# A new emission order, explicit waits at the port that VectorE and GpSimd share, and a plan that keeps DMA issue and DMA data apart, in a fused local-attention and feed-forward kernel

## The chip, the cores and the metric

The kernel runs on one core of a Trainium2 chip. The metric is the device time of one execution in microseconds (us); lower is better. A core has five engines that run instruction streams of their own: TensorE (PE, matmuls), VectorE (DVE), ScalarE (ACT), GpSimd (POOL) and SyncE (SP). In this kernel SyncE computes nothing: it issues every DMA. Engines wait for each other through semaphores.

## What is computed

```python
B, H, S, D = q.shape
block, window = (32, 16)
...
k_sum = k.reshape(B, H, nb, block, D).max(axis=3)
v_sum = v.reshape(B, H, nb, block, D).mean(axis=3)
scores_l = scale * np.matmul(q, k.transpose(0, 1, 3, 2))
...
mask_l = np.abs(pos[:, None] - pos[None, :]) < window
scores_s = scale * np.einsum('bhsd,bhnd->bhsn', q, k_sum)
scores_s = scores_s + np.log(block)
scores_l_m = np.where(mask_l, scores_l, -1000000000.0)
scores_all = np.concatenate([scores_l_m, scores_s], axis=-1)
...
a = a / (np.sum(a, axis=-1, keepdims=True) + 1e-09)
v_all = np.concatenate([v, v_sum], axis=2)
return np.matmul(a, v_all).astype(np.float32)
...
h = x @ w_in
g = h * (1.0 / (1.0 + np.exp(-h)))
return (g @ w_out).astype(np.float32)
```

There are 4 batches, 8 heads, 768 tokens and 64 elements in a head; `a` is the exponential of the scores less their maximum.

The attention output, laid out as 3072 tokens by 512, is the input x of the feed-forward part (FFN). All data is float32.

## The kernel before

**Work and tiles.** Products are made in float16: each float32 operand is split into a high part and a rest, and a product takes three matmuls (high by high, high by low, low by high). The attention runs in 24 tiles (4 batches times 6) of 128 tokens; each tile is worked on in score groups `m` of two heads. A score group is: matmuls q by keys into one PSUM bank (L665, L666), masking, scaling and row maximum on VectorE (L677), exponentials on ScalarE (L680), the reciprocal of the sum on VectorE (L696, L697), a scaled copy `p` in float16 on any of three engines (L702 ScalarE, L704 GpSimd, L706 VectorE), its float16 rest on VectorE (L715, four instructions), a transposing DMA `tt<-p` (L718), and the product with the values (L751). The inputs are split beforehand: keys and queries by L554/L555 and L559/L560, values in `job_vs`: a transfer `raw<-in_v`, two small transfers of the block means `raw<-vms` (L613), a scaling of `raw` (L616 ScalarE or L617 GpSimd), the high half `vv` (L247 or L249), and the rest `vv` (L265, VectorE or GpSimd).

The FFN runs in chunks of 256 tokens and slices of the 2048 features: `ffn1` (L897, 24 matmuls of 256 columns), then `t` (L911 ScalarE, L912 VectorE), the high half of `g` (L916 ScalarE), its rest (`less`, L265, VectorE or GpSimd), and two groups of six matmuls `ffn2` (L906). PE is kept busy by placing FFN groups between the score groups of the attention.

**What sets the order.** The class `Plan` collects 2528 operations with the engines that each may run on, a cost for each and their data dependencies. The order and the engine of every operation are written out in the string `ORDER` (three characters each). `replay()` walks through it and gives each operation a planned start and stop; operations that use the port which VectorE and GpSimd share (`port`) are planned one after the other, over both engines. DMAs go in the plan on an engine "dma", which is SyncE's queue. `issue()` then emits the operations sorted by planned start, and chains the instructions of each engine in that order. The planned times set the order alone; on the chip each engine runs its own chain, and waits only for data, for buffers and for the engine itself. SyncE holds up to eight direct transfers in flight: the next one's wait (`DMAHW0` to `DMAHW7`) is on the one eight before it. At the start, before the first products are ready, PE runs `fills`, throw-away matmuls on `ident` (L378).

## Time and profile before

| | |
|---|---|
| median of 3 runs | 622.41 us (621.0 to 623.33) |
| the profiled execution | 621.28 us, span 619.6 us |
| granted TensorE clock | 1.00 over the span |
| PE busy | 607.1 us, 98% |
| VectorE busy | 481.9 us, 78% |
| ScalarE busy | 394.8 us, 64% |
| GpSimd busy | 150.4 us, 24% |

Times in the trace count from the first instruction of the span. An idle time in brackets is what an engine stood still just before the instruction, and behind the arrow stands what it waited for last. Instructions of one engine overlap a little at their ends, so one row may start before the row above it has stopped.

### The profile page before, as it was taken

The numbers are of one execution on the slowest core, as the hardware profiler recorded it, in microseconds if no ns is written. First come the engines' busy times: TensorE is split into PE (matmuls) and PEld (weight loads), VectorE is DVE, ScalarE is ACT, GpSimd is POOL, SyncE is SP. The second block draws the span as 40 slices with busy tenths as digits, with TensorE's granted clock in tenths as the row PEclk, the third lists the DMA queues.
The fourth block names the chain that finished last, engine by engine and source line by source line (L and its number), as shares of the span: only waits on it lengthen the run. The fifth ranks groups of instructions, "written<-read, shape, count | busy, mean of one in ns | idle before, by whom it ended". The sixth has DMA issues, their size and how long they took to land. (4 is left out here: it accounts for less than half of the span.)

```text
span 619.6 us, 13715 instructions
## 1 busy us (share of the span) xinstructions
PE 607.1 (98%) x5086; PEld 427.9 (69%) x5086; DVE 481.9 (78%) x1371; ACT 394.8 (64%) x870; POOL 150.4 (24%) x181
## 2 busy tenths in 40 slices
PE   8999999999999999999999999999999999999997
PEld 5776666676776676767766666666667777667775
DVE  7999999999899757997889855898878886754122
ACT  4989998577767658565866556655776556542321
POOL 1445662032321223013212031320222123200200
PEclk9999999999999999999999999999999999999999
DMA  9989626554763873864653874655455654312000
GB/s 315 331 308 393 241 87 161 136 148 123 176 176 72 225 209 100 202 143 108 187 147 101 171 205 142 170 157 144 87 159 125 142 131 98 60 26 60 35 2 35
DMA packets 91559, 93.49 MB, mean 151 GB/s; under 512 B 70348, under 2 KB 72652, under 8 KB 89444
## 3 DMA queue, kind: packets, MB, share of 16 engines
q1 hardware_dynamic: 91492, 92.62, 53.9%
q8 instruction: 40, 0.66, 0.4%
q14 instruction: 27, 0.22, 0.1%
HBM read 68.12 MB, written 6.29 MB: 120 GB/s over the span
## 5 line engine op out<-in xcount | busy, mean ns | idle before, releaser
L906 PE MATMUL bank<-wt,g 128*128 128x512 f16 (+2 forms) x1168 | 277.9, 382 | 0.8 <-ACT g L916 0.7
L897 PE MATMUL bank<-xh,wt 128*128 128x256 f16 x1536 | 274.4, 273 | 0.0
L897 PEld LDWEIGHTS <-wt 128*128 128x128 f16 x2304 | 224.2, 98 | 46.1 <-issue 4.0
L897 PE MATMUL bank<-xl,wt 128*128 128x256 f16 x768 | 209.3, 273 | 0.0
L906 PEld LDWEIGHTS <-g 128*128 128x128 f16 x1104 | 106.5, 98 | 97.2 <-DVE g L265 1.0
L911 ACT ACTIVATE t<-bank,asc 128x512 f32<-128x512 f32 x96 | 65.6, 683 | 87.5 <-PE bank L897 86.7
L912 DVE SCALAR_TENSOR_TENSOR t<-t,bank 128x512 f32<-128x512 f32 x96 | 65.5, 682 | 50.0 <-ACT t L911 49.1
L680 ACT ACTIVATE e<-e,mx 128x182 f32<-128x182 f32 x192 | 83.8, 438 | 26.4 <-DVE mx L677 25.2
L265 POOL TENSOR_TENSOR g<-t,g 128x512 f16<-128x512 f32 x38 | 47.5, 1249 | 195.2 <-ACT g L916 176.3
L715 DVE SCALAR_TENSOR_TENSOR p<-e,sum,p 128x128 f16<-128x128 f32 x320 | 89.7, 342 | 5.6 <-ACT p L702 4.3
L916 ACT CAST g<-t 128x512 f16<-128x512 f32 x88 | 54.0, 614 | 45.7 <-DVE t L912 43.7
L677 DVE CUSTOM_DVE_ANT_0 e<-bank,masks,qsc 128x182 f32<-128x182 f32 x144 | 54.2, 402 | 17.7 <-PE bank L666 15.6
L704 POOL TENSOR_SCALAR p<-e,sum 128x182 f16<-128x182 f32 x47 | 22.9, 490 | 127.3 <-DVE sum L697 48.4
L265 DVE TENSOR_TENSOR g<-t,g 128x512 f16<-128x512 f32 x50 | 34.9, 698 | 11.8 <-ACT g L916 11.8
L702 ACT ACTIVATE p<-e,sum 128x182 f16<-128x182 f32 x68 | 28.4, 438 | 17.5 <-issue 8.4
L680 ACT ACTIVATION_READ_ACCUMULATOR e<-e,mx 128x1 f32 x192 | 36.2, 188 | 0.0
L665 PE MATMUL bank<-qk 128*128 128x182 f16 x144 | 28.7, 241 | 4.8 <-DVE mx L677 3.3
L560 DVE SCALAR_TENSOR_TENSOR qk<-raw,qsc,qk 64x1264 f16<-64x1264 f32 x18 | 27.6, 1534 | 3.6 <-ACT qk L559 3.1
L666 PE MATMUL bank<-qk 128*128 128x182 f16 x144 | 28.7, 242 | 0.0
L559 ACT ACTIVATE qk<-raw,qsc 128x1264 f16<-128x1264 f32 x18 | 24.1, 1341 | 5.9 <-DMA raw<-in_kD_dram 5.9
L265 POOL TENSOR_TENSOR vv<-raw,vv 128x1024 f16<-128x1024 f32 x9 | 19.4, 2155 | 28.0 <-ACT vv L247 24.2
L751 PE MATMUL bank<-tt,vv 128*64 128x128 f16 x800 | 24.4, 220 | 0.0
(168 smaller groups left out, 661.2 us busy)
## 6 DMA issues: line engine op xcount, KB each, us to landing
wt<-in_w_dram SPq DMA_DIRECT2D x16, 1024.0 KB
raw<-in_kD_dram SPq DMA_DIRECT2D x18, 632.0 KB
raw<-in_v_dram SPq DMA_DIRECT2D x20, 512.0 KB
raw<-in_qD_dram SPq DMA_DIRECT2D x18, 512.0 KB
out_dram<-raw SPq DMA_DIRECT2D x23, 256.0 KB
raw<-in_kF_dram SPq DMA_DIRECT2D x12, 384.0 KB
raw<-in_qF_dram SPq DMA_DIRECT2D x9, 512.0 KB
raw<-in_vR_dram SPq DMA_DIRECT2D x12, 384.0 KB
```

The lines of the kernel that those rows point to most:

```text
L265: eng[e].tensor_tensor(out=out, in0=in0, in1=in1, op=ALU.subtract)
L665: nc.tensor.matmul(out=sc[:, i, :NKEY], lhsT=qh[:, h, :], rhs=kst[:, h, :], start=True, stop=False)
L666: nc.tensor.matmul(out=sc[:, i, :NKEY], lhsT=ql[:, h, :], rhs=kst[:, h, :], start=False, stop=True)
L677: plan.op({"dve": 258 if b == 0 else 323}, lambda e, i=i: nc.vector.tensor_tensor_reduce(out=et[:, i, :NKEY], in0=sc[:, i, :NKEY], in1=mas ...
L680: plan.op({"act": 431}, lambda e, i=i, h=h: nc.scalar.activation(out=et[:, i, :NKEY], in_=et[:, i, :NKEY], func=AF.Exp, scale=-1.0, bias=m ...
L702: nc.scalar.activation(out=out, in_=et[:, i, :NKEY], func=AF.Copy, scale=by)
L715: nc.vector.scalar_tensor_tensor(out=pt[:, i, to:to + z - a], in0=et[:, i, a:z], scalar=su[:, i:i + 1], in1=pt[:, i, a:z], op0=ALU.mult, o ...
L897: nc.tensor.matmul(out=h[:, d * CH:(d + 1) * CH], lhsT=wt[f, 0][:, part, d, ct * P:(ct + 1) * P], rhs=x[:, ct, :], start=(ct == 0 and q == ...
L906: nc.tensor.matmul(out=bank[to][:, :z0 - a0], lhsT=a[:, d * CH + u * P:d * CH + u * P + P], rhs=b[:, d, a0:z0], start=(opens and d == 0 an ...
L911: plan.op({"act": 640}, lambda e: nc.scalar.activation(out=t, in_=h, func=AF.Tanh, scale=asc_t[c // 3 % 2][:, f:f + 1]), r=[("bank", k), ( ...
L912: plan.op({"dve": 605}, lambda e: nc.vector.scalar_tensor_tensor(out=t, in0=t, scalar=1.0, in1=h, op0=ALU.add, op1=ALU.mult), r=[("bank", ...
L916: plan.op({"act": 540}, lambda e: nc.scalar.copy(out=gh, in_=t), r=[("t", j)], w=[("gh", n)], prio=at - TUNE["post"])
```

## The change

Four things change.

1. **Plan, transfers.** `replay()` keeps two times for a DMA: how long SyncE's queue is held (`cols`, default `ISSUE` = 380 ns, more for transposes, small transfers and pairs), and how long the data path is (`moved`). Before, one cost stood for both. The costs of some transfers change, and the plan's first DMA is possible at 800 ns and not at 2100.
2. **Wait.** `issue()` remembers in `held` VectorE's last instruction that uses the shared port. A GpSimd operation that uses it, is planned to take over 400 ns and starts less than 4000 ns behind the planned stop of that instruction gets a semaphore wait for it. Each `held` is used once.
3. **A new `ORDER`** of the same 2528 operations with the same dependencies. 191 of them are on another engine. Of the 88 FFN rests `g` (L265), GpSimd has 31 and VectorE 57 (before 38 and 50); of the value operations `vv`, GpSimd has 22 (16), VectorE 11 (16).
4. As a result of 1 and 3, other `fills`: 47 and not 48.

97 of GpSimd's 148 operations carry the new wait, among them 20 of the 31 `g`. Line numbers of the new kernel are 11 higher from `job_k` on.

```diff
-    DMA0 = 2100.0
+    DMA0 = 800.0
+    ISSUE = 380
...
+        if "dma" in engines:
+            cols = cols or self.ISSUE
         self.ops.append((engines, fn, sorted(deps), prio, cols, port))
...
-            t = max([free.get(e, 0.0), shared if e in port else 0.0] + [end[d] + self.lag(chosen[d], e) for d in deps])
+            t = max([free.get(e, 0.0), shared if e in port else 0.0] + [end[d] + self.lag(chosen[d], e) - (self.LEAD if e == "dma" else 0) for d in deps])
...
+            elif e == "dma":
+                stop = moved = max(t + self.LEAD, moved) + cost
             else:
                 stop = t + cost
-            end[i], chosen[i], free[e] = stop, e, stop
+            end[i], chosen[i], free[e] = stop, e, t + cols if e == "dma" else stop
...
-        for _, _, i, e, fills in sorted(self.schedule(), key=lambda o: o[0]):
+        for t, stop, i, e, fills in sorted(self.schedule(), key=lambda o: o[0]):
...
+            port = e in self.ops[i][5]
             for ins in traced[seen:]:
+                if port and e == "pool" and stop - t > 400 and held and t - held[1] < 4000:
+                    self.tc.add_manual_dep(ins, held[0], mybir.DependencyInfo(mybir.DependencyClass.Sync, mybir.DependencyReason.DATA), reason="port")
+                    held = None
...
+                if port and e == "dve":
+                    held = ins.name, stop
...
-        plan.op({"dma": 800}, vm, r=["vms"], w=key, prio=prio)
+        plan.op({"dma": 480}, vm, r=["vms"], w=key, prio=prio, cols=1520)
...
 ORDER = (
-    "00l0071lu00b00r00h01f01k01p00402005p06q06w05w06606207007606c01501b02401t02807800v07g01106e02y06m03902j07i02f07p07v0av0aq"
...
```

**Place 1, SyncE's queue near the start.** `in_w` are slices of the FFN weights (1 MB each; `wt_74` is the one that the first score group of the trace waits for), `in_q0` and `in_v` inputs, `vms` the block means, which ScalarE must have made. Before:

```order
L537 DMA qk0_137<-in_q0_dram 128x256 [waits DMAHW3_49]
L609 DMA raw2_136<-in_v_dram 128x1024 [waits DMAHW4_49]
L805 DMA wt_66<-in_w_dram 128x2048 [waits DMAHW5_49]
L537 DMA qk1_138<-in_q0_dram 128x256 [waits DMAHW6_49,PE_49]
L574 DMA wt_76<-vms_148 24x512 [waits DMAHW7_49,Activation_49]
L805 DMA wt_65<-in_w_dram 128x2048 [waits DMAHW0_49]
L805 DMA wt_72<-in_w_dram 128x2048 [waits DMAHW1_49]
L574 DMA wt_77<-vms_148 24x512 [waits DMAHW2_49]
L805 DMA wt_74<-in_w_dram 128x2048 [waits DMAHW3_49]
L537 DMA qk1_138<-in_q0_dram 128x256 [waits DMAHW4_49]
```

After:

```order
L816 DMA wt_66<-in_w_dram 128x2048 [waits DMAHW3_49]
L816 DMA wt_65<-in_w_dram 128x2048 [waits DMAHW4_49]
L584 DMA wt_77<-in_v_dram 30x512 [waits DMAHW5_49]
L585 DMA wt_76<-vms_148 24x512 [waits DMAHW6_49,Activation_49]
L816 DMA wt_72<-in_w_dram 128x2048 [waits DMAHW7_49]
L584 DMA wt_76<-in_v_dram 30x512 [waits DMAHW0_49]
L585 DMA wt_77<-vms_148 24x512 [waits DMAHW1_49]
L816 DMA wt_74<-in_w_dram 128x2048 [waits DMAHW2_49]
L548 DMA qk1_138<-in_q0_dram 128x256 [waits DMAHW3_49,PE_49]
L620 DMA raw2_136<-in_v_dram 128x1024 [waits DMAHW4_49]
```

`wt_66` and `wt_65` now go ahead of the first `vms` transfer, and the transfers to `raw2_136` (512 KB) and `qk1_138` (128 KB), which stood ahead of `wt_74`, now stand behind it.

**Place 2, GpSimd and VectorE where batch 2 is prepared (326 us of the trace).** `p` are scaled probabilities, `vv` the rests of values, `g` those of the FFN. GpSimd before:

```order
L704 TENSOR_SCALAR p_170<-e1_161,sum1_155 128x182 [waits DMAHW6_49,DVE_49,Activation_49]
L249 TENSOR_SCALAR qk1_138<-ks_140 128x8x24 [waits PE_49]
L265 TENSOR_TENSOR vv0_152<-raw2_136,vv0_152 128x1024 [waits DMAHW5_49,DMAHW6_49,DMAHW2_49,Activation_49]
L265 TENSOR_TENSOR g1_186<-t0_183,g1_186 128x512 [waits Activation_49]
L704 TENSOR_SCALAR p_170<-e1_161,sum1_155 128x182 [waits DMAHW3_49,Pool_49]
```

VectorE before, around the same point:

```order
L259 TENSOR_SCALAR asc0_92<-ur_91,vsc0_150 128x8
L715 SCALAR_TENSOR_TENSOR p_170<-e2_162,sum2_156,p_170 128x128 [waits DMAHW4_49,Activation_49]
L715 SCALAR_TENSOR_TENSOR p_170<-e2_162,sum2_156,p_170 128x54
L715 SCALAR_TENSOR_TENSOR p_170<-e2_162,sum2_156,p_170 128x128
L715 SCALAR_TENSOR_TENSOR p_170<-e2_162,sum2_156,p_170 128x54
L677 ISA e2_162,mx2_159<-bank6_194,masks_133,qsc0_143 128x182 [waits DVE_49,PE_49]
L677 ISA mx2_159 128x1
L677 ISA e2_162,mx2_159<-bank6_194,masks_133,qsc0_143 128x182 [waits DVE_49]
L677 ISA mx2_159 128x1
```

GpSimd after:

```order
L715 TENSOR_SCALAR p_170<-e1_161,sum1_155 128x182 [waits DMAHW0_49,DMAHW7_49,DVE_49,Activation_49]
L715 TENSOR_SCALAR p_170<-e1_161,sum1_155 128x182 [waits DMAHW5_49,DVE_49]
L276 TENSOR_TENSOR vv0_152<-raw2_136,vv0_152 128x1024 [waits DMAHW2_49,DMAHW3_49,DVE_49,Activation_49]
L276 TENSOR_TENSOR g1_186<-t0_183,g1_186 128x512 [waits Activation_49,Pool_49]
L268 TENSOR_SCALAR asc0_92<-ur_91,vsc0_150 128x8
```

VectorE after:

```order
L726 SCALAR_TENSOR_TENSOR p_170<-e0_160,sum0_154,p_170 128x128 [waits DMAHW4_49,DVE_49,Activation_49]
L726 SCALAR_TENSOR_TENSOR p_170<-e0_160,sum0_154,p_170 128x54
L726 SCALAR_TENSOR_TENSOR p_170<-e0_160,sum0_154,p_170 128x128
L726 SCALAR_TENSOR_TENSOR p_170<-e0_160,sum0_154,p_170 128x54
L717 TENSOR_SCALAR p_170<-e1_161,sum1_155 128x182 [waits DMAHW5_49]
L688 ISA e2_162,mx2_159<-bank6_194,masks_133,qsc0_143 128x182 [waits DVE_49,PE_49]
L688 ISA mx2_159 128x1
```

The `vv` operation now waits for VectorE too (`DVE_49`): for the L717 row, which stands behind the L726 rows and ahead of the first L688.

**Place 3, ScalarE where batch 3 is prepared (432 us).** `raw<-raw,vsc` is the scaling of the values. ScalarE before:

```order
L916 CAST g0_185<-t1_184 128x512
L255 ACTIVATE xh1_180<-bank3_191 128x4x128
L255 ACTIVATE xh1_180<-bank7_195 128x4x128
L616 ACTIVATE raw0_134<-raw0_134,vsc1_151 128x1024
L680 ACTIVATE e0_160,sum0_154<-e0_160,mx0_157 128x182 x2
L680 ACTIVATE e1_161,sum1_155<-e1_161,mx1_158 128x182 x2
L911 ACTIVATE t0_183<-bank0_188,asc0_92 128x512
```

ScalarE after:

```order
L927 CAST g0_185<-t1_184 128x512
L266 ACTIVATE xh1_180<-bank3_191 128x4x128
L266 ACTIVATE xh1_180<-bank7_195 128x4x128
L691 ACTIVATE e0_160,sum0_154<-e0_160,mx0_157 128x182 x2
L922 ACTIVATE t0_183<-bank0_188,asc0_92 128x512
L266 ACTIVATE raw1_135<-bank5_193,osc0_98 128x512
L691 ACTIVATE e1_161,sum1_155<-e1_161,mx1_158 128x182 x2
```

GpSimd after:

```order
L276 TENSOR_TENSOR g0_185<-t1_184,g0_185 128x512 [waits PE_49,DVE_49,Activation_49,Pool_49]
L628 TENSOR_SCALAR raw0_134<-raw0_134,vsc1_151 128x1024 [waits DMAHW4_49,DMAHW5_49,DMAHW3_49,DMAHW6_49,DMAHW1_49,DVE_49]
L260 TENSOR_SCALAR vv0_152<-raw0_134 128x1024 [waits PE_49,Pool_49]
```

The scaling has left ScalarE, ahead of four exponentials (L680, now L691), and is now the second of these GpSimd rows, with the new wait for VectorE.

## Rows read from the trace of the kernel before

**Rows 1.** The page, part 1: busy time of each engine, instructions.
```profile
PE 607.1 (98%) x5086; PEld 427.9 (69%) x5086; DVE 481.9 (78%) x1371; ACT 394.8 (64%) x870; POOL 150.4 (24%) x181
```
**Rows 2.** Waits of PE: us in total, times, longest.
```profile
PE bank L665 <- DVE mx L677: 3.3, 3, 1.5
...
PE bank L689 <- ACT e L680: 0.3, 1, 0.3
```
**Rows 3.** Timeline of PE: start, length, work [idle before <- what ended it].
```profile
34.79 1.27 PE L378 MATMUL bank<-ident 128*128 128x256 bf16 x10
37.14 0.53 PE L660 MATMUL bank<-wt,qk 64*128 64x158 f32 x2 [1.08 <-ACT wt L247]
...
322.61 0.24 PE L665 MATMUL bank<-qk 128*128 128x182 f16 x1 [0.95 <-DVE mx L677]
...
329.59 0.24 PE L665 MATMUL bank<-qk 128*128 128x182 f16 x1 [1.45 <-DVE sum L697]
...
361.38 0.60 PE L906 MATMUL bank<-wt,g 128*128 128x512 f16 x2 [0.66 <-ACT g L916]
...
390.46 0.25 PE L665 MATMUL bank<-qk 128*128 128x182 f16 x1 [0.88 <-DVE mx L677]
...
434.95 0.24 PE L665 MATMUL bank<-qk 128*128 128x182 f16 x1 [1.49 <-DVE mx L677]
```
**Rows 4.** Timeline of ScalarE and of SyncE's queue near the start.
```profile
34.43 1.16 ACT L815 ACTIVATE wt<-wt 128x1024 f32<-128x1024 f32 x1 [1.72 <-DMA wt<-in_w_dram]
...
20.91 0.86 SPq L574 DMA_DIRECT2D wt<-vms  x1
```
**Rows 5.** Stretches: busy by engine (instructions), clock, DMA share, GB/s.
```profile
20.00:22.00 2.00, 2.00 (x17) 1.66 (x16) 1.97 (x6) 2.00 (x6) 0.00 (x0) 1.00 0.55 216
22.00:24.00 2.00, 2.00 (x35) 1.84 (x34) 1.86 (x10) 1.91 (x3) 1.14 (x1) 1.00 0.63 120
24.00:26.00 2.00, 2.00 (x33) 1.71 (x33) 2.00 (x11) 1.84 (x9) 0.00 (x0) 1.00 1.00 414
```
**Rows 6.** Timeline of ScalarE, VectorE and SyncE where late data held an engine.
```profile
317.01 1.35 ACT L559 ACTIVATE qk<-raw,qsc 128x1264 f16<-128x1264 f32 x1 [2.57 <-DMA raw<-in_kD_dram]
...
350.74 2.60 SPq L718 DMA_TRANSPOSE tt<-p  x2
353.38 0.58 SPq L428 DMA_DIRECT2D raw<-in_kF_dram  x1
...
358.89 0.95 DVE L429 TENSOR_REDUCE km<-raw 128x24 f32<-128x768 f32 x1 [4.52 <-DMA raw<-in_kF_dram]
...
431.75 1.15 ACT L616 ACTIVATE raw<-raw,vsc 128x1024 f32<-128x1024 f32 x1 [2.74 <-DMA raw<-vms]
```
**Rows 7.** Timeline of VectorE and GpSimd at two score groups that came late.
```profile
324.91 0.99 DVE L715 SCALAR_TENSOR_TENSOR p<-e,sum,p 128x128 f16<-128x128 f32 x4
...
325.95 2.85 DVE L715 SCALAR_TENSOR_TENSOR p<-e,sum,p 128x128 f16<-128x128 f32 x4
...
326.06 2.22 POOL L265 TENSOR_TENSOR vv<-raw,vv 128x1024 f16<-128x1024 f32 x1 [11.12 <-ACT vv L247]
...
387.60 1.89 DVE L715 SCALAR_TENSOR_TENSOR p<-e,sum,p 128x128 f16<-128x128 f32 x4
...
388.04 1.36 POOL L265 TENSOR_TENSOR g<-t,g 128x512 f16<-128x512 f32 x1 [5.24 <-ACT g L916]
```
**Rows 8.** Timeline of GpSimd and VectorE: a `g` operation beside a maximum of scores.
```profile
486.12 1.16 POOL L265 TENSOR_TENSOR g<-t,g 128x512 f16<-128x512 f32 x1 [4.60 <-ACT g L916]
...
486.97 0.41 DVE L677 CUSTOM_DVE_ANT_0 e<-bank,masks,qsc 128x182 f32<-128x182 f32 x1 [0.88 <-PE bank L666]
```
**Rows 9.** The page, part 5: the rests `g` on either engine.
```profile
L265 POOL TENSOR_TENSOR g<-t,g 128x512 f16<-128x512 f32 x38 | 47.5, 1249 | 195.2 <-ACT g L916 176.3
...
L265 DVE TENSOR_TENSOR g<-t,g 128x512 f16<-128x512 f32 x50 | 34.9, 698 | 11.8 <-ACT g L916 11.8
```
**Rows 10.** A stretch of 20 us early in the kernel, columns as in Rows 5.
```profile
120.00:140.00 20.00, 20.00 (x183) 14.57 (x178) 19.43 (x58) 12.86 (x32) 4.75 (x6) 1.00 0.61 167
```

More of the change, by code (lines that the diff above doesn't have):

```diff
@@ L176, in replay @@
         end, chosen, order = {}, {}, []
-        free, shared, seen, filled = {"dma": self.DMA0}, 0.0, {}, self.FIRST
+        free, shared, seen, filled, moved = {"dma": self.DMA0}, 0.0, {}, self.FIRST, 0.0
         for k in range(0, len(ORDER), 3):
@@ L226, in issue @@
     def issue(self):
-        last, seen = {}, 0
-        for _, _, i, e, fills in sorted(self.schedule(), key=lambda o: o[0]):
+        last, seen, held = {}, 0, None
+        for t, stop, i, e, fills in sorted(self.schedule(), key=lambda o: o[0]):
             for _ in range(fills):
@@ L427, in job_k @@
                     nc.vector.memset(band[:, 0, :HALO], NEG)
-            plan.op({"dma": 1020}, lambda e, kf=kf, hp=hp: nc.sync.dma_start(out=kf, in_=kF[b, :, hp, :]), w=key, prio=prio)
+            plan.op({"dma": 1080}, lambda e, kf=kf, hp=hp: nc.sync.dma_start(out=kf, in_=kF[b, :, hp, :]), w=key, prio=prio)
             plan.op({"dve": 869}, lambda e, kf=kf, hp=hp: nc.vector.tensor_reduce(out=km[:, hp, :], in_=kf.rearrange("p (n k) -> p n k", k=BLK), axis=AX.X, op=ALU.max),
@@ L467, in job_km @@
             for u in range(2):
-                plan.op({"dma": 400}, lambda e, hh=hh, u=u: nc.sync.dma_start(out=kd_t[u * 64:u * 64 + 64, :, hh, :], in_=km[hh * 64:hh * 64 + 64]),
-                        r=[("km", hp) for hp in range(4)], w=[("kd", hh, u)], prio=prio)
+                plan.op({"dma": 240}, lambda e, hh=hh, u=u: nc.sync.dma_start(out=kd_t[u * 64:u * 64 + 64, :, hh, :], in_=km[hh * 64:hh * 64 + 64]),
+                        r=[("km", hp) for hp in range(4)], w=[("kd", hh, u)], prio=prio, cols=650)
         kd = [("kd", hh, u) for hh in range(2) for u in range(2)]
@@ L572, in side_v @@
         vr, key = plain_v[t]
-        plan.op({"dma": 400}, lambda e: nc.sync.dma_start(out=vr[:NSIDE, 1, :], in_=v[0, t, :NSIDE, 1, :]), w=key[1:], prio=prio)
-        plan.op({"dma": 400}, lambda e: nc.sync.dma_start(out=vr[NSIDE:NS2, 1, :], in_=vms_t), r=["vms"], w=key[1:], prio=prio)
+        plan.op({"dma": 320}, lambda e: nc.sync.dma_start(out=vr[:NSIDE, 1, :], in_=v[0, t, :NSIDE, 1, :]), w=key[1:], prio=prio)
+        plan.op({"dma": 240}, lambda e: nc.sync.dma_start(out=vr[NSIDE:NS2, 1, :], in_=vms_t), r=["vms"], w=key[1:], prio=prio, cols=760)
     def job_mean(prio):
@@ L717, in job_a @@
         plan.op({"dve": 900}, low, r=er + sums, w=[("p", pk), ("p", pk, "half")], prio=prio)
-        plan.op({"dma": 672}, lambda e: nc.sync.dma_start_transpose(out=tt, in_=pt.rearrange("p a b -> p (a b)")), r=[("p", pk), ("p", pk, "half")], w=[ttk], prio=prio)
+        plan.op({"dma": 672}, lambda e: nc.sync.dma_start_transpose(out=tt, in_=pt.rearrange("p a b -> p (a b)")), r=[("p", pk), ("p", pk, "half")], w=[ttk], prio=prio, cols=1230)
     def job_c(m, prio):
@@ L1080 @@
[L1080 to L1083 removed]
+    "1lw00700l00r1lz00b00h01f01k00405p02401p02f01t05w02801507006q06206600v01b07601106c06e0av06w06m02j03d02u07807g07i02n07z085"
@@ new lines @@
+    "07p0aq0b907v08708t08z08j08p08f09103s0430bq0bg0b00bm09i0ck0bw09n0cq02y0re0320980rl0ca03o0d20200cg0dj0dp0by0d90df0ed0e30e9"
+    "03903h0ga0rr0ru0ej0f203w04904d05g0dr0dz0rz0s40el0et04g04n0f70c604s04x09s0fc0520gf09x0tm0tt0sx0cs0570d00fh0m40gt0ha0hg05c"
+    "0s70se0hu0i00h00i40a00a70tz0h60u20ia05l09b0ac0sl0sp0hi0hq0ic0st0u70ik0im0j30ta0jx0fk0fr0jn0t410a0it0gk0ai0ao10h0b50ev0j9"
+    "12i0k30jt0k50iz0td12p0tj0km0jb0jj0kr0kw0uc0uf0l10kc0l40lu12v0fw0lc0g210l10q1nh0um11t1250ux10v0lz0md0no0ne0nu0mu0n00gp0kf"
@@ new lines @@
+    "0g81cw1nm0mk1nu0mq0n212y0nk0nw0v51md0v10n91mk0lg1201d10vi0o40vc1d91290vu0w11dd0o60on0w70od0p71dj1dv1e00oj1dl0ph0pd0pn0ot"
+    "0pp0wa0wg0ur1e80vl0ov0q60wk0wn0qb0qg0pw0p30wu0x50xd0xq0x10y21n41dq0y91ec0lm0m91uz0pz0ql0qo1mt12f0yd0x91eu0qw0yi1101ei0ls"
+    "1uw1ez0xk1f70yn14q14x0ys0yv0r00r61330z21ne1up1411ek1ep1fb1fh1nz1v71ud1690zd1530xt0z70vr16g0ra13a11311a1560zh14814e1vy1w4"
+    "14h1fo0zl0zx1h216y1h71hf0zs1751hj1hp1o215b16m1ft1fy1fj1g61mn13b15g1um1ga17b1hw13i15j1j010118h18s18o1wa17e1gg1gn0xz16p107"
@@ L1084 @@
+    "9f39f99gf9gn9gr9ff9fl9g29gx8zx9hj9ho9hw9h19fg9fs9h99he9is9ix9i09i69ia9j59j99jf9ii9in9jj9h49k19id9jr9k69jw9la9ke9ki9jm9ko"
+    "9lf9ln9lr9ku9l09l59mj9mo9lx9m19m99me9kv9fw8zn9mw9ns9n09n69na9ni9nx9o59o99nn9p19of9p69m49nd9pe9oj9om9pi9po9ps9or9pv9qd9g6"
+    "9q09qn9qq9ow9qg9q59qx9r0"
 )
```

115 lines of the change are left out of this document (52 added, 63 removed).

## The prediction

> **What bounds the kernel now.** I read the page first, then the waits of TensorE (PE), then its timeline at each wait, then the other engines there. The page gives PE 607.1 us busy in a span of 619.6 [rows 1], so PE is the bound, and all that an order can win is in its 12.5 idle us. The changed kernel issues the same matmuls but for one throw-away. The list of PE's waits has few rows: scores that wait for VectorE, 3.3 us in three waits, down to one of 0.3 for an exponential [rows 2]. The timeline puts places to them: 1.08 us at 37.14, before the first score group, and five stops later, 0.95, 1.45, 0.66, 0.88 and 1.49 [rows 3], in sum 5.43. The rest, 12.5 - 1.08 - 5.43 = 6.0 us, is the first start, small holes of the start-up, and the time after PE's last matmul, in which the last output is evicted and stored; nothing in the change shortens that. The reader is to see that no single engine is short over the whole; PE is stopped at six places, each by one thing that came late.
>
> **The start: new order of SyncE's queue.** At 37.14 the score group waited for ScalarE, which itself had stood 1.72 us for a slice of the weights [rows 4]; PE had already run ten throw-away matmuls (1.27 us, 0.13 each) [rows 3]. The slice, `wt_74`, was late because SyncE stood at a `vms` transfer issued at 20.91 [rows 4], and the data path was used at a share of 0.55 and 0.63 for 4 us, where 1.00 was to be had right behind [rows 5]. Place 1 of the order shows two slices pulled ahead of that wait, and 0.64 MB put behind `wt_74`. At the 414 GB/s of the full stretch [rows 5], 0.64 MB is 1.5 us, and the two half-empty stretches hold 2 x 0.45 + 2 x 0.37 = 1.6 us more. Either is more than 1.08, so this stop should go whole; with one throw-away less (0.13) the gain is **1.2 us**. It is no more, since those throw-aways that remain are in the order and cost what they cost. Bounds: 0 (the slice lands as before, for instance because the next thing late is the `vms` transfer itself) to 1.2. I take 1.2, as two independent causes each suffice.
>
> **Late data in the middle: 0.95 + 0.66 + 1.49 = 3.10 us.**
> - At 322.61 the score group came late since ScalarE's L559, which stood 2.57 us for `raw<-in_kD`, ran at 317.01 ahead of work that VectorE's queue needed [rows 6]. In the new order the score group stands behind further FFN work (one `ffn2` group and a value product); each PE group placed there covers over 1 us, more than 0.95.
> - At 361.38 `ffn2` waited for `g`: VectorE had stood 4.52 us at L429 for `raw<-in_kF`, issued at 353.38 behind two transposes that held the queue for 2.60 [rows 6]. The new order issues it ahead of these two, and 2.6 exceeds 0.66.
> - At 434.95 ScalarE's scaling L616 (1.15 us) stood for `raw<-vms` 2.74 us, with four exponentials behind it [rows 6]. Place 3 of the order shows it on GpSimd, behind which no exponential stands. The stop was 1.49 of those 2.74; the exponentials are free of all of it. What is late next is the value operation itself on GpSimd, whose reader, a value product, comes later on PE.
>
> The plan's separation of issue and data time costs nothing by itself: it decides the order, and the transfers and their number are the same. Its effect is the three items above.
>
> **The port: 1.45 + 0.88 = 2.33 us.** At 326.06 GpSimd began a `vv` operation of 2.22 us, 0.11 us into VectorE's four L715 instructions. These took 2.85 us; the four just before took 0.99 [rows 7]. VectorE lost 1.86 us, and the score group behind it came 1.45 late. At 388.04 a `g` operation began amid four L715 that took 1.89, so 0.90 lost, against a stop of 0.88 [rows 7]. Place 2 of the order shows the `vv` operation made to wait for VectorE's L717, that is behind all eight L715 and directly ahead of the score maxima (L677). A maximum reads scores from PSUM, and beside GpSimd it ran unstretched, 0.41 us at 486.97 with a `g` operation from 486.12 for 1.16, itself below its mean of 1.249 [rows 8, 9]. So there the GpSimd operation lies where it costs nothing, and both stops go. The `g` operation of the second place gets a wait on the same group of four. Bounds: 0 to 2.33; I take 2.33.
>
> The Trainium skill (SBUF — State Buffer, Who interferes with whom) says that the shared ports are an exclusive lock: whoever issues first keeps it for its whole instruction, and the other is blocked fully. By that rule the wait removes no blocking, it only chooses who blocks whom, and the next VectorE instruction with two SBUF inputs behind the GpSimd operation would pay. The trace agrees with the lock (1.86 of 2.22 lost, 0.90 of 1.36) and, at 486.97, with the page's exemption of an instruction that has at most one input in SBUF. If the blocking were only handed on, the 2.33 would stay and the sum would be 2.3 higher.
>
> **What the new wait adds.** 97 GpSimd operations wait. Behind a waiting one stand GpSimd's next operations: scaled `p`, whose readers are L715 and the transposes, and `g`, read by `ffn2`. No row of PE's waits names GpSimd's `g` or `vv`, although `g` takes 1.249 us there and 0.698 on VectorE [rows 9], so PE's queue has room for that difference at least. The plan already kept users of the port apart, so a wait bites only where the chip differs from the plan. GpSimd is 24% busy [rows 1], and its queue has no backlog. The 20 `g` with a wait are those that could hurt: 0 each if the wait was met, one VectorE operation each (0.698, the nearest row) if not; 0 to 14.0 us in sum. I take 0 for the sum, by the absent PE waits, and keep the end for a rival.
>
> **Operations on another engine.** Seven `g` less on GpSimd and more on VectorE, 7 x 0.698 = +4.9 us on VectorE; five `vv` less on it, about 1.2 us each by a VectorE instruction of twice the size of `g` (0.698 x 2 less its start), -6. VectorE is as full as before, and that is the cost: early on it is 19.43 of 20 us busy [rows 10], so a small error has nowhere to go.
>
> **New stops.** The old order was made for PE to be fed, and five stops were left. The new one is unproven on the chip in the same way: I put one stop of the largest kind (1.49) and one of the smallest (0.3) [rows 2, 3], **+1.8 us**, a third of 5.43; bounds 0 and 5.4.
>
> **Sum.** -1.2 - 3.10 - 2.33 + 1.8 = -4.8 us: 621.28 becomes 616.5. The profiled execution was 1.13 us below the median of 622.41, so the forecast for the median is 622.4 - 4.8 = **617.6 us**. 0.5% of the time is 3.1 us, about what a measurement can tell from no change: faster means below 619.3, slower above 625.5.
>
> **Rivals.**
> - *The collisions are handed on.* A waiting GpSimd operation starts right behind one L715 group and lies beside the next VectorE instruction that can be stretched; the scores behind that one come late instead. The 2.33 then stay: 617.6 + 2.3 = 619.9. For it: the two rows of stretched L715 [rows 7], and VectorE with hardly a gap early on [rows 10]. Against: at both places score maxima follow, and one ran unstretched [rows 8]. The skill's rule above asks for this one. No change by my bound; 0.07.
> - *The middle is rebuilt.* Every change of order makes new coincidences, the six places are healed and others open at the same rate: the middle stays at 5.4, only the start wins. 622.4 - 1.2 = 621.2 us. For it: VectorE's load early on [rows 10]. Against: each of the five has a cause that the order rows or the waits take away. No change by my bound; 0.16.
> - *It does not do what it says.* The slice lands when it did (the queue waits for `vms` anyway), transfers come as before, the GpSimd waits are all met already: then only the two stops healed by order alone go, 0.95 and 1.49, 622.4 - 2.4 = 620.0. For it: ScalarE must have made `vms` in either order. Against: the half-empty data path [rows 5]. No change; 0.05.
> - *Slower: the waits hold `g`.* GpSimd's `g` starts a VectorE operation later, `ffn2` waits for it, PE stands. From 6.63 + 3.1 = 9.7 us of new idle on, that is 0.49 per waiting `g`, the kernel is slower by the bound; with all 20 by 0.698, 622.4 - 6.6 + 14.0 = 629.8 us. For it: a wait is paid even if the port would have been free. Against: PE never waits for `g` on GpSimd now. 0.10.
>
> **How the numbers follow.** The forecast with its spread (615.5 to 619.3) has 0.62. Its low end is the sum without new stops, 622.4 - 6.6 = 615.8, with 0.3 for the scatter. Faster 0.62. Same: 0.07 + 0.16 + 0.05, and 0.02 of the waits' rival where they bite little, 0.30. Slower 0.08. The range reaches over the rebuilt middle: 615.5 to 621.8; left out are the slower rival and the ends of the others.
>
> **What would show it.** In the changed profile: no stop before the first score group at 37 us, a DMA share near 1.00 from 20 to 24 us, and four L715 beside a `vv` at about 1 us and not 2.85. PE's waits should hold less than 2 us in the middle. A row of PE waiting for GpSimd's `g` or for `vv` would speak for the slower rival; as many waits for VectorE's maximum as before, for the rebuilt middle. Wrong I would be above all if PE's busy time itself grew, which nothing here lets me expect.

## The result and the profile after

The changed kernel takes 612.45 us in the median of four runs (611.96 to 613.45), the kernel before 622.87 (621.0 to 624.52): a ratio of 0.9836, with an interval of 0.9804 to 0.9867. The profiled execution took 612.63 us with a span of 610.9, against 621.28 and 619.6. That is 10.4 us by the medians and 8.7 by the spans; forecast were 4.8, and the time lies under the range. The direction and most places were right, the size was not.

The page of the changed kernel, busy times and instructions, answers to [rows 1]:

```profile
PE 605.8 (99%) x5085; PEld 427.6 (70%) x5085; DVE 466.9 (76%) x1384; ACT 391.5 (64%) x866; POOL 139.7 (23%) x172
```

TensorE's (PE's) idle time is 610.9 - 605.8 = 5.1 us and not 12.5. VectorE is 15 us less busy and GpSimd 10.7. 191 of the 2528 operations are on another engine, but that is not what does it: the same order without the wait shows 480.9 and 150.0 (new_no_wait below). The list of PE's waits, complete but for what is too small to be listed, answers to [rows 2]:

```profile
PE bank L389 <- POOL ident masks.py:199: 1.4, 1, 1.4
PE bank L671 <- DVE km L440: 0.3, 1, 0.3
PE bank L746 <- DMA wt<-vms: 0.2, 1, 0.2
```

Nothing behind 40 us is left in it: no wait for VectorE's maxima and none for GpSimd (the one for GpSimd's `ident` is at 1.43 us). The places of [rows 3] and [rows 7] look so, in the timelines of PE, VectorE and GpSimd:

```profile
34.48 1.27 PE L389 MATMUL bank<-ident 128*128 128x256 bf16 x10
35.68 0.55 PE L671 MATMUL bank<-wt,qk 64*128 64x158 f32 x4
...
321.58 1.97 DVE L726 SCALAR_TENSOR_TENSOR p<-e,sum,p 128x128 f16<-128x128 f32 x8
323.47 0.31 DVE L717 TENSOR_SCALAR p<-e,sum 128x182 f16<-128x182 f32 x1
323.88 0.41 DVE L688 CUSTOM_DVE_ANT_0 e<-bank,masks,qsc 128x182 f32<-128x182 f32 x1
...
323.91 2.13 POOL L276 TENSOR_TENSOR vv<-raw,vv 128x1024 f16<-128x1024 f32 x1 [1.79 <-DVE p L717]
...
381.25 0.98 DVE L726 SCALAR_TENSOR_TENSOR p<-e,sum,p 128x128 f16<-128x128 f32 x4
...
382.40 1.16 POOL L276 TENSOR_TENSOR g<-t,g 128x512 f16<-128x512 f32 x1 [2.34 <-ACT qk L258]
```

The throw-aways run into the first score group without a stop. The eight L726 take 1.97 us, 0.99 for four, where four took 2.85 [rows 7]; the `vv` operation stands behind L717, as its row says, beside the maxima, which take 0.41.

One expected sign did not come. The DMA share from 20 to 24 us was to be near 1.00; it is 0.80 and 0.72 (0.55 and 0.63 before [rows 5]). SyncE still issues its first `vms` at 20.88 us (20.91 before [rows 4]), and `wt_74` is issued when it was. Two stretches of the changed kernel, then the row of `wt_74`, after and before:

```profile
20.00:22.00 2.00, 2.00 (x17) 1.66 (x16) 2.00 (x4) 2.00 (x6) 0.00 (x0) 1.00 0.80 323
22.00:24.00 2.00, 2.00 (x38) 1.87 (x38) 1.79 (x17) 2.00 (x4) 0.11 (x1) 1.00 0.72 147
...
23.62 0.52 SPq L816 DMA_DIRECT2D wt<-in_w_dram  x1
...
23.63 0.52 SPq L805 DMA_DIRECT2D wt<-in_w_dram  x1
```

So the slice is not asked for earlier, and yet ScalarE no longer waits for it. What differs is what lies ahead of it in the queue: 0.64 MB now stands behind it, and `wt_65` and `wt_66` went ahead of the `vms` wait.

**Where the time went.** The table compares the two kernels at points where they have done the same PE work. It gives the end of that work in the two traces; the shift between two lines is what was won in between.

| PE work done up to | before, us | after, us | shift | won here | idle shown there before |
|---|---|---|---|---|---|
| behind the first score group | 38.89 | 36.86 | -2.02 | 2.02 | 1.08 and 0.29 |
| 312 us of before | 311.60 | 309.72 | -1.89 | -0.13 | |
| 333 us | 332.98 | 328.38 | -4.60 | 2.71 | 0.95 + 1.45 = 2.40 |
| 371 us | 370.98 | 365.35 | -5.63 | 1.03 | 0.66 |
| 399 us | 399.08 | 392.40 | -6.68 | 1.05 | 0.88 |
| 449 us | 449.39 | 441.02 | -8.36 | 1.68 | 1.49 |
| start of the last 48 matmuls | 608.24 | 599.88 | -8.36 | 0 | |
| end of the span | 619.6 | 610.9 | -8.7 | 0.3 | |

Nearly everything was won where the six stops were, nothing came back elsewhere, and the five stops in the middle were worth more than the idle time that their rows show: 6.47 us and not 5.43. Each kernel has one trace here, and the stops differ between traces of the old order (see old_new_plan): a single line of the table carries that scatter, their sum less.

### The profile page after: what moved, and what is told of

Its sections match the earlier page's. It is cut to its first block, busy times and chain, and to the rows that moved or that the text cites. A ratio compares the mean times of both kernels' runs of the same rounds, so it can differ in the third digit from the quotient of the medians.

```text
span 610.9 us, 13765 instructions
## 1 busy us (share of the span) xinstructions
PE 605.8 (99%) x5085; PEld 427.6 (70%) x5085; DVE 466.9 (76%) x1384; ACT 391.5 (64%) x866; POOL 139.7 (23%) x172
## 4 chain that ended last, share of the span: by engine, by line
PE 94%; DMA 3%; ACT 1%; SPq 0%; DVE 0%; issue 0%
PE bank L917 42%; PE bank L908 41%; PE bank L762 4%; PE bank L676 2%; PE bank L677 2%; DMA wt<-in_w_dram 1%; DMA wt<-in_kF_dram 1%; PE bank L746 1%; DMA wt<-vms 1%; PE bank L674 1%; PE bank L671 0%; ACT wt L826 0%; ACT e L691 0%; PE bank L389 0%; PE bank L460 0%
## 5 line engine op out<-in xcount | busy, mean ns | idle before, releaser
L691 ACT ACTIVATE e<-e,mx 128x182 f32<-128x182 f32 x192 | 83.8, 438 | 29.2 <-DVE mx L688 28.9
L726 DVE SCALAR_TENSOR_TENSOR p<-e,sum,p 128x128 f16<-128x128 f32 x320 | 80.1, 313 | 2.9 <-POOL p L715 1.7
L276 POOL TENSOR_TENSOR g<-t,g 128x512 f16<-128x512 f32 x31 | 35.9, 1158 | 161.3 <-ACT g L927 77.5
L688 DVE CUSTOM_DVE_ANT_0 e<-bank,masks,qsc 128x182 f32<-128x182 f32 x144 | 54.0, 402 | 21.0 <-PE bank L677 19.0
L715 POOL TENSOR_SCALAR p<-e,sum 128x182 f16<-128x182 f32 x45 | 24.6, 549 | 119.1 <-DVE sum L708 23.5
L276 DVE TENSOR_TENSOR g<-t,g 128x512 f16<-128x512 f32 x57 | 39.7, 696 | 12.0 <-ACT g L927 11.3
L691 ACT ACTIVATION_READ_ACCUMULATOR e<-e,mx 128x1 f32 x192 | 36.1, 188 | 0.0
L713 ACT ACTIVATE p<-e,sum 128x182 f16<-128x182 f32 x65 | 26.6, 437 | 14.1 <-DVE sum L708 7.4
L276 POOL TENSOR_TENSOR vv<-raw,vv 128x1024 f16<-128x1024 f32 x12 | 25.6, 2133 | 15.6 <-DVE p L717 5.9
L677 PE MATMUL bank<-qk 128*128 128x182 f16 x144 | 28.7, 242 | 0.0
L566 DVE SCALAR_TENSOR_TENSOR qk<-raw,qsc,qk 128x1024 f16<-128x1024 f32 x18 | 23.7, 1316 | 3.7 <-ACT qk L565 3.6
```

What stands on the lines that cost most here:

```text
L276: eng[e].tensor_tensor(out=out, in0=in0, in1=in1, op=ALU.subtract)
L677: nc.tensor.matmul(out=sc[:, i, :NKEY], lhsT=ql[:, h, :], rhs=kst[:, h, :], start=False, stop=True)
L688: plan.op({"dve": 258 if b == 0 else 323}, lambda e, i=i: nc.vector.tensor_tensor_reduce(out=et[:, i, :NKEY], in0=sc[:, i, :NKEY], in1=mas ...
L691: plan.op({"act": 431}, lambda e, i=i, h=h: nc.scalar.activation(out=et[:, i, :NKEY], in_=et[:, i, :NKEY], func=AF.Exp, scale=-1.0, bias=m ...
L726: nc.vector.scalar_tensor_tensor(out=pt[:, i, to:to + z - a], in0=et[:, i, a:z], scalar=su[:, i:i + 1], in1=pt[:, i, a:z], op0=ALU.mult, o ...
```

## The experiments

All kernels were timed against the kernel before on the same chip; the ratio is to it, and the median stands beside that of the kernel before, timed with it. Three chips were used, and the median of the kernel before differs between them. The ratio is not the quotient of the two medians. kf_early, start_dma, new_start and new_start_wait run through the new plan, so old_new_plan is what their traces are best held against.

| kernel | median, us | before, us | ratio (interval) | VectorE, GpSimd busy, us |
|---|---|---|---|---|
| old_new_plan | 622.12 | 622.0 | 0.9997 (0.9978 to 1.0017) | 482.0, 149.3 |
| start_dma | 621.51 | 622.89 | 0.998 (0.9961 to 0.9999) | |
| new_start | 619.05 | 622.0 | 0.995 (0.993 to 0.997) | 480.6, 147.9 |
| kf_early | 622.0 | 622.37 | 0.9988 (0.9966 to 1.001) | 481.7, 149.6 |
| old_wait_vv | 621.44 | 622.37 | 0.9969 (0.9952 to 0.9987) | 480.9, 149.4 |
| old_wait_two | 618.41 | 622.37 | 0.9934 (0.9908 to 0.9959) | 477.5, 149.1 |
| old_wait | 617.76 | 622.0 | 0.993 (0.9907 to 0.9952) | 470.2, 139.0 |
| new_start_wait | 615.99 | 622.89 | 0.9896 (0.9871 to 0.9922) | 470.1, 143.2 |
| new_no_wait | 617.55 | 622.0 | 0.9926 (0.9898 to 0.9953) | 480.9, 150.0 |
| wait_short | 617.65 | 622.89 | 0.9917 (0.9892 to 0.9942) | 481.3, 144.2 |
| wait_long | 612.34 | 622.89 | 0.9844 (0.9817 to 0.9871) | 467.2, 141.4 |
| wait_all | 613.03 | 622.37 | 0.9833 (0.9802 to 0.9863) | 467.1, 137.6 |

### The parts, alone and without

**The plan.** The old `ORDER` in the changed `replay()`, no wait:

```diff
 ORDER = (
-    (the new string)
+    (the string of before)
...
-                if port and e == "pool" and stop - t > 400 and held and t - held[1] < 4000:
-                    self.tc.add_manual_dep(ins, held[0], ...)
-                    held = None
```

> The old order run through the new plan (issue and data time of transfers apart, new costs), without the wait. Each engine's instructions stand in the same order as before, but one throw-away matmul at the start stands elsewhere. Theory (the plan's times act only through the order that was made with them): 622.9 us, within 0.5, all six stops as before. Rival (the plan's times change something by themselves): over 1 us to either side. It also gives the scatter of the old order between runs: 621.0 to 624.5 in four runs before, against 612.0 to 613.5 of the changed kernel.

0.9997 (0.9978 to 1.0017): the plan's separate times do nothing that this shows. They were of use in making the order.

The expected "all six stops as before" did not come. VectorE, ScalarE, GpSimd and SyncE run the same instructions in the same order as before and the span is the same (619.5 and 619.6), but the trace has no stop ahead of the first score group and none at 361.38; instead PE stands 0.5 and 0.4 us at an `ffn1` and 0.4 for a `g` on GpSimd. The slice landed 0.7 us earlier than before from the same queue. Rows of ScalarE and of PE:

```profile
33.74 1.18 ACT L823 ACTIVATE wt<-wt 128x1024 f32<-128x1024 f32 x1 [0.89 <-DMA wt<-in_w_dram]
...
36.45 0.53 PE L668 MATMUL bank<-wt,qk 64*128 64x158 f32 x2
```

kf_early has the same two stops missing. In the traces with the old order of the start, the stop of 1.08 is 0 (old_new_plan, kf_early), 0.32, 0.54 and 0.71 (the three old_wait kernels). A stop that is gone in one trace of a changed kernel is therefore not yet cured by the change.

**The wait alone.** The kernel before with the new `issue()` and nothing else:

```diff
+                if port and e == "pool" and stop - t > 400 and held and t - held[1] < 4000:
+                    self.tc.add_manual_dep(ins, held[0], ...)
+                    held = None
...
+                if port and e == "dve":
+                    held = ins.name, stop
```

> The kernel before with its old order, plan and fills, and the new wait alone. Theory (parts add up): the stops at 329.59 (1.45) and 390.46 (0.88) go, the four others stay, 622.9 - 2.3 to 2.7 = 620.2 us; DVE's busy time falls by some 15 us as in the changed kernel (481.9 to 466.9). Rival A (the wait needs an order made for it: GpSimd's g and vv come later and PE waits for them): slower than 622.9 us, with rows of PE waiting for GpSimd. Rival B (no influence): 622.9 us, with the same stops.

It wins 4.2 us, half again as much as the 2.7 that were expected. Neither rival holds: behind the start no PE wait names GpSimd. Page and PE's waits of old_wait (its lines are 6 higher than before):

```profile
PE 606.9 (99%) x5086; PEld 427.9 (70%) x5086; DVE 470.2 (76%) x1371; ACT 395.3 (64%) x870; POOL 139.0 (23%) x181
...
PE bank L671 <- DVE mx L683: 1.0, 1, 1.0
PE bank L912 <- ACT g L922: 0.7, 1, 0.7
```

Of the middle stops two are left, those at 322.61 and 361.38 of before. Three are gone, and one of them is the stop at 434.95, which the prediction had put down to late data. With the same instructions in the same order VectorE is 11.7 us less busy (15 were expected) and GpSimd 11.4: the time that the two lose to each other is not handed from one to the other, it goes on both.

**The order without the wait.** The changed kernel less the three lines of the wait:

```diff
-                if port and e == "pool" and stop - t > 400 and held and t - held[1] < 4000:
-                    self.tc.add_manual_dep(ins, held[0], ...)
-                    held = None
```

> The changed kernel with its new order and fills, but without the new wait of GpSimd for VectorE: 97 waits fewer, nothing else. Theory (the parts add up; the wait is what removed the two stops by port collisions): GpSimd's vv operation near 326 us and the g operation near 388 us start amid L715 groups again, PE stands there about 1.5 and 0.9 us again, and the time is 612.5 + 2.4 to 2.9 = 615 us or a little over. Rival A (the order alone did it; the waits were met when reached): 612.5 us, within 0.5, and no stop of PE in the middle. Rival B (the waits cost, hidden so far): 611.5 us or less. Rival C (collisions reach PE at many places without the waits): above 617 us, with more than three waits of PE for VectorE.

617.55, so the wait is worth 5.1 us in the new order by the medians and 4.2 by the spans: Rival C. The way it loses them is not that of the old order, though. There is no long stop; at 30 us PE is 0.7 us ahead of the changed kernel, and then it falls behind in a dozen steps of 0.1 to 0.75 us between 33 and 462 us, to 4.2 at the end. Behind the first start its longest listed wait is 0.7 us, for VectorE:

```profile
PE bank L845 <- DVE wm L847: 1.0, 2, 0.7
PE bank L457 <- DVE qm L449: 0.7, 2, 0.5
PE bank L673 <- DVE mx L685: 0.4, 1, 0.4
PE bank L914 <- POOL g L273: 0.3, 1, 0.3
```

### Which waits carry it

**By length.** The condition `stop - t > 400` of the changed kernel becomes `stop - t > 1000` (wait_long) or `1000 >= stop - t > 400` (wait_short).

> The changed kernel with the new wait only on GpSimd operations that the plan gives over 1000 ns (g, vv, scalings, weight splits), and not on the scaled p of 427. Theory (a collision costs VectorE about as much as the GpSimd operation is long, as 1.86 of 2.22 and 0.90 of 1.36): long ones carry nearly all, 612.5 to 613.5 us. Rival (the many short ones carry it, 45 scaled p that stand close to L726, which is most often what is stretched): 615 us or more.

> The complement of wait_long: the new wait only on GpSimd operations of 400 to 1000 ns in the plan, the scaled p. Theory (length decides): close to the kernel without any wait, 617 us. Rival (the many short ones carry it): 613 to 614 us. If both parts together give more or less than the whole 5.1 us, an operation that is made to wait changes where the next one falls.

612.34 and 617.65: the whole gain hangs on the operations planned over 1000 ns, and the scaled `p` carry none. The length theory holds.

**Two places of the old order.** The wait only at the operations of [rows 7]:

```diff
-                if port and e == "pool" and stop - t > 400 and held and t - held[1] < 4000:
+                if i in (1409, 1900) and port and e == "pool" and held and t - held[1] < 4000:
```

> The kernel before with the new wait at two GpSimd operations only, the two of the prediction: the vv operation at 326.06 us and the g operation at 388.04. Theory of the prediction (a collision costs what the stop behind it shows): the stops at 329.59 and 390.46 go, 2.33 us as shown and 2.7 with PE's refill, 622.4 - 2.7 = 619.7 us, the stop at 434.95 stays. Rival (collisions are carried on through late VectorE work to stops far behind): the stop at 434.95 shrinks too, 618 us.

Two waits win 4.0 us by the medians (618.41), as good as all of them in the old order. Measured at the same PE work, the stops of before at 329.59 and 390.46 give 1.61 and 1.05; 1.51 more come at 434.95, 47 us behind the second wait. The rival holds: a collision is carried on. The second wait in fact takes two collisions away: VectorE comes early enough to be through with the scale L464 (L458 before) at 389.54, 0.9 us before the `vv` operation begins that had met it.

**One place.** The wait only at the `vv` operation at 390.87 us, `i in (1678,)`.

> The kernel before with the new wait at one GpSimd operation only, the vv operation at 390.87 us, during which a VectorE instruction on 128x1 elements (L458, a scale of the queries) took 1.95 us and not 0.14, with no stop of PE near it. Theory (lateness is carried): the scales, the transposes and then in_v and vms in SyncE's queue come about 1 us earlier, and the stop at 434.95, 44 us later, shrinks from 1.49 to under 0.5; 622.4 - 1.2 = 621.2 us. Rival (that stop comes from the order of transfers and of ScalarE alone, as the prediction has it): the stop is there as before, 622.4 us.

The stop at 434.95 shrinks to 0.62, and by the medians 0.9 us are won, a ratio clear of 1. Timelines of VectorE, GpSimd, SyncE and ScalarE, first before:

```profile
390.87 2.13 POOL L265 TENSOR_TENSOR vv<-raw,vv 128x1024 f16<-128x1024 f32 x1 [1.46 <-ACT vv L247]
...
391.06 1.95 DVE L458 SCALAR_TENSOR_TENSOR qsc<-qc 128x1 f32<-128x1 f32 x1
392.94 0.15 DVE L459 SCALAR_TENSOR_TENSOR qsc<-qsc 128x1 f32<-128x1 f32 x1
...
424.45 0.57 SPq L609 DMA_DIRECT2D raw<-in_v_dram  x1
428.63 1.65 SPq L613 DMA_DIRECT2D raw<-vms  x2
```

Then old_wait_vv:

```profile
392.54 0.14 DVE L464 SCALAR_TENSOR_TENSOR qsc<-qc 128x1 f32<-128x1 f32 x1
...
393.84 2.13 POOL L271 TENSOR_TENSOR vv<-raw,vv 128x1024 f16<-128x1024 f32 x1 [3.22 <-PE bank L903]
...
428.80 2.04 SPq L619 DMA_DIRECT2D raw<-vms  x2
...
435.51 0.24 PE L671 MATMUL bank<-qk 128*128 128x182 f16 x1 [0.62 <-DVE mx L683]
```

And old_wait_two at the same ScalarE instruction (L616 before, L622 here):

```profile
425.50 1.64 SPq L619 DMA_DIRECT2D raw<-vms  x2
...
428.61 1.15 ACT L622 ACTIVATE raw<-raw,vsc 128x1024 f32<-128x1024 f32 x1 [1.54 <-DVE masks L481]
```

A scale of one number per partition took 1.95 us beside a 128x1024 operation of GpSimd and 0.14 without. (The `vv` row names PE; VectorE's last L721 before it had ended at 393.71.) No PE wait follows the scale for 44 us, so the prediction's list of stops could not show it. The reading is that from the scale on the score work, the transposes and SyncE's queue were late, and 41 us on ScalarE stood for `vms` with exponentials behind it. In old_wait_two ScalarE no longer waits for the transfer there.

How far is this shown? The whole trace of old_wait_vv lies 1.44 us later than before at 425 us, by its start (last section), so `vms` has to be held against PE's work. Put so, its pair is fully issued earlier than before by 0.12 us (start_dma), 0.27 (kf_early), 0.60 (old_new_plan), 0.82 (new_start), 0.88 (old_wait_vv), 1.00 (new_start_wait), 1.46 (old_wait) and 1.63 (old_wait_two), and the stops are 1.38, 1.25, 0.91, 0.67, 0.62, 0.39, none and none: the stop shrinks by what `vms` gains. But the first four have no wait, and the `vv` operation costs VectorE 1.8 to 1.9 us in each, if at another instruction (L467, 128x1, in old_new_plan; one of four L723 in start_dma):

```profile
391.01 2.04 DVE L467 SCALAR_TENSOR_TENSOR qsc<-qsc 128x1 f32<-128x1 f32 x1
...
389.54 2.85 DVE L723 SCALAR_TENSOR_TENSOR p<-e,sum,p 128x128 f16<-128x128 f32 x4
```

So the same collision goes with stops from 0.67 to 1.49, and the 0.62 of one trace lies only just below. That late `vms` sets the stop is shown. That this one collision makes part of its lateness is supported by the medians and by the two kernels in which the stop is gone, but not settled, and 0.62 is left without it.

**All port operations.** The changed kernel with `if port and e == "pool" and held:`.

> The changed kernel with the wait for every GpSimd operation that uses the port, short ones and those planned later than 4000 ns too. Theory (the long ones carry all): 612.4 us, within 0.5. Rival (some collisions are left that a wait can take away): below 611.9 us, with VectorE less busy than 466.9. Second rival (a wait costs something at small operations): above 613 us.

613.03, ratio 0.9833, VectorE 467.1: as the changed kernel. The median lies a hair over the line of the second rival, but two of the five runs had a granted clock of 0.997, and the spans are 610.5 and 610.9. Nothing is left to win this way, and no kernel here is clearly faster than the changed one.

### The order's own part

**The start.** The new order for 200 operations, up to the first score group, then the old one, no wait; `ORDER` is the first 200 entries of the new string, then all others as they stand in the old one.

> The new order up to the first score group at about 36 us (200 of 2528 operations), the old order and engines behind it, no wait. Theory (the start is a gain of its own, 2.0 us in the two traces by where the same PE work stands): 622.9 - 2.0 = 620.9 us, with all five stops of the middle still there, shifted by 2 us. Rival (what the start gains is used up at the next late thing, so the start pays only together with the rest): 622.9 us, with new stops between 37 and 320 us.

619.05, so 2.95 us by the medians and 2.4 by the spans, and the middle stops are there as before. The start is a gain of its own.

**Three transfers of it.** Only SyncE's queue is changed, in the old order (through the new plan):

```diff
-L609 DMA raw2<-in_v, L805 DMA wt_66<-in_w, L537 DMA qk1<-in_q0, L574 DMA wt_76<-vms, L805 wt_65, L805 wt_72, L574 wt_77<-vms, L805 wt_74
+L805 DMA wt_66<-in_w, L805 wt_65, L574 DMA wt_76<-vms, L805 wt_72, L574 wt_77<-vms, L805 wt_74, L537 DMA qk1<-in_q0, L609 DMA raw2<-in_v
```

> The kernel before with three transfers of SyncE's queue moved and nothing else: raw2<-in_v and one qk1<-in_q go from ahead of the weight slices to behind wt_74, and wt_65 goes ahead of the first vms transfer. No wait, old order on all other engines, the throw-aways as in the kernel old_new_plan. Theory (the first score group was late because its slice of weights landed late): ScalarE no longer waits for the slice at 34 us, the stop at 37 us goes, 622.0 - 1.2 to 2.0 = about 620.4 us. Rival (the start's gain of 2.95 in new_start is from the moved work of ScalarE, VectorE and GpSimd, and the slice is late by other things): 622.0 us, within 0.5, with the stop still there.

The slice is on time. ScalarE's row has no idle time (it was 1.72 [rows 4]), and the score group no stop:

```profile
32.47 1.14 ACT L823 ACTIVATE wt<-wt 128x1024 f32<-128x1024 f32 x1
...
36.38 0.55 PE L668 MATMUL bank<-wt,qk 64*128 64x158 f32 x4
```

0.998 is 1.25 us, the 1.2 of the prediction, but the interval reaches from 0.06 to 2.4 us, and the missing stop proves little, since old_new_plan lacks it with the old queue. That ScalarE no longer waits for the slice does speak for the transfers: it waited 1.72, 0.89 and 0.69 us in before, old_new_plan and kf_early. The other 1.7 of new_start by the medians must come from what else it moves, other transfers and the work of the other engines; which of them is not shown.

**One transfer in the middle.** `raw<-in_kF` of batch 3 is moved in SyncE's queue from behind two transposes to ahead of them (old order, new plan).

> The kernel before with one transfer moved in SyncE's queue, raw<-in_kF of batch 3, ahead of the two transposes that stood before it (350.74, 2.60 us); no wait. Theory of the prediction: the transfer lands about 2.6 us earlier, VectorE's L429 no longer holds t and g, the stop at 361.38 (0.66, 0.88 with the refill) goes, 622.1 - 0.9 = 621.2 us, with the other stops as before. Rival (the transposes behind it come late and with them a value product): a new stop between 355 and 372 us of 0.5 or more, 622 us.

Inconclusive. 0.9988 with an interval over 1 can't tell 0.9 us from nothing. The stop of 361.38 isn't among this kernel's PE waits, but in old_new_plan, with the transfer in its old place, PE has no idle time at that work either; and kf_early has a wait of 0.4 for `qm` that old_new_plan lacks.

**Start and wait together.**

> The new order up to the first score group, the old order behind it, and the new wait. If the start (2.95 by new_start) and the waits (4.25 by old_wait) add up: 622.0 - 7.2 = 614.8 us; less 0.9 of it if both heal the same stop at 37 us, as old_wait's trace has that stop 0.93 us smaller: 615.7 us. What is then left to the changed kernel's 612.5 is what the order behind the start is worth beside the waits, 2.3 to 3.2 us, by the two stops of data at 321 and 360 us, which old_wait still shows (1.0 and 0.7). Rival (the order behind the start is worth nothing beside the waits): 612.5 us.

615.99, 6.9 us under the kernel before; 2.95 and 4.24 apart make 7.2. So the two share 0.3 us by the medians (1.0 by the ratios); the expected 0.9 can't be told from either. PE's waits behind 40 us show what is left for the rest of the order:

```profile
PE bank L676 <- DVE mx L688: 1.7, 2, 1.3
...
PE bank L917 <- ACT g L927: 1.1, 1, 1.1
PE bank L460 <- DVE qm L452: 0.3, 1, 0.3
```

They are at 321, 431, 359 and 375 us: the two stops by late transfers (1.3 and 1.1) and two small ones. 3.1 shown, and 3.5 from 615.99 to 612.45.

So the parts are 6.9 us for the start and the wait together (about 3.0 and 4.2 alone) and 3.5 for the rest of the order, 10.4 in all.

## Why the prediction was wrong in size

The step that failed most is **New stops**: 1.8 us were taken off the gain by analogy with the old order, and there was no new stop. Next come three terms that were too small: the shown idle times stood for the loss (5.43 us; it was 6.47), the start (1.2; 2.0 in the traces) and the end (0; 0.3). Together the four make 3.9 us, from the forecast 4.8 to the 8.7 of the traces; the medians add 1.7.

- **What bounds the kernel: right.** Six stops of PE were nearly all that was won, and all of them went. Only "in its 12.5 idle us" was too narrow: of the 8.7 us PE's idle time gave 7.4 and its busy time 1.3, with one throw-away (0.13) less. The stops reach into what is shown as busy (below).
- **The start, 1.2: half right in cause, too small.** Of the two causes that were each to suffice, the half-empty data path was filled by less than half (0.80 and 0.72 from 20 to 24 us) and the slice was not issued earlier; what is left is the 0.64 MB and the order of the slices. start_dma measures 1.25 for the transfers alone, loosely, and the 1.08 was the largest that any trace with the old start shows. The start as a whole gave 2.0 between the traces: two smaller things that I saw as "small holes" are in it, a stop of 0.3 for an exponential [rows 2], and first scores that were issued in pieces (from their first matmul to the next work 1.67 us before, 1.11 after).
- **The port, 2.33 and its cause: right.** Both stops go with two waits alone (old_wait_two). What was wrong is the step from a collision to the stop behind it alone. Work that PE did not need until 47 us later was late too. Most of the wait's 4.2 us beyond my 2.33 is that: 1.56 at 434.95 in the trace of old_wait.
- **Late data, 3.10: one of three wrong in cause.** The stop at 434.95 was put down to ScalarE's place in the order [rows 6]; it is gone with ScalarE's order as it was (old_wait, old_wait_two). The row's releaser, `raw<-vms`, was true but not the beginning of the chain. The transfer itself was late, and the waits at the port alone bring it forward; the collision 41 us ahead of it is the likeliest beginning, not a proven one. The other two stops need the order: they stand in old_wait and new_start_wait. That a further PE group (321) or the earlier `kF` (361) heals them is argued, not shown, since kf_early doesn't settle it.
- **The size of a stop: the idle time in a row is less than the loss.** 5.43 shown were 6.47 in the table. PE's matmuls follow each other at 0.11 us (the last two rows before the stop at 329.59), but each is shown for 0.27:

```profile
327.76 0.27 PE L897 MATMUL bank<-xl,wt 128*128 128x256 f16 x1
327.87 0.27 PE L897 MATMUL bank<-xh,wt 128*128 128x256 f16 x1
329.59 0.24 PE L665 MATMUL bank<-qk 128*128 128x182 f16 x1 [1.45 <-DVE sum L697]
```

  From start to start it is 1.72 us; less 0.11, 1.61 were lost and not 1.45, and 1.61 is what old_wait_two won there. Five stops at about 0.2 make the 1.04. The figure was in the rows before.
- **New stops, +1.8: wrong, the largest single term.** There was none. They were put in by analogy with the old order. new_no_wait shows what would have made them: without the wait the new order loses 4.2 us in small steps. The order and the wait were weighed apart, and their effect on each other was not: with the collisions taken away the new order ran on the chip without a stop.
- **The end, 0: 0.3 us,** the last store; not traced further.
- **The level.** The forecast was set against a median of 622.41, and the profiled execution of before lay 1.1 below it; with the later run its median is 622.87, 1.6 over that execution, while the changed kernel's profiled execution lies 0.2 over its own. That makes 10.4 us by the medians where the traces have 8.7; where the scatter comes from stands below. Of the misses 1.8 + 1.0 + 0.8 + 0.3 = 3.9 us are terms of the sum, and the rest, 1.7, is this.
- **The rivals.** "The collisions are handed on" fell with the busy times of old_wait, where both engines win. There the Trainium skill (SBUF — State Buffer, Who interferes with whom) says that whoever issues first keeps the ports and the other is blocked. L458, 1.95 us beside a 2.13 us operation that began 0.19 us before it, is that rule as it stands. What I had added to it, that blocking is only passed on, is not in the trace: behind the awaited VectorE operation there often stand readers of PSUM. Maxima run beside GpSimd's operations of over 1 us for 19.3 us in the changed trace (L688), 8.0 before (L677). "The middle is rebuilt" would have come nearer without the wait, though 617.55 is not its 621.2, and "the waits hold `g`" has no row: PE never waits for `g` on GpSimd in the changed kernel.

## What to carry to other kernels

A list of waits of the bounding engine shows where lateness arrives, not where it is made. And one trace is not enough: three of the six stops came and went, or changed by half, between traces of the old order. Before a late transfer is put down to its place in a queue, follow the side engines back, tens of microseconds if need be, to an instruction that took many times what its like takes. And two waits at the right places were worth as much as all of them in the old order: in an in-order engine that shares a port, let the long operation wait for a stretch in which the other reads elsewhere.
